# A column transform by one step of radix two, and the order of an opening: a float32 FFT and MoE kernel

## The chip, the cores and the metric

The kernel runs on one core of one Trainium2 chip. The metric is the device time in microseconds (us) of one execution; a kernel's time is the median of its runs. All arithmetic is in float32.

## The reference

```python
X = np.fft.fft(x, axis=1)          # x: (8, 3008, 256) float32
X = np.fft.fft(X, axis=2)
x = X.real.reshape(24064, 256)
h = x @ w_in                       # (256, 2048)
g = h * np.cos(h)
out = g @ w_out                    # (2048, 256)
```

A two-dimensional Fourier transform of each of 8 batches is taken, its real part goes through two matrix products with h cos(h) between them.

## The kernel before, in words

The transform along the 3008 rows is done in two halves with matrices of cosines and sines; the transform along the 256 columns is not applied to the data at all but to w_in, once, in the opening of the kernel. This folded w_in has two parts, WC (cosines, e = 0) and WS (sines, e = 1), 128 x 2048 each, and it takes the place of w_in for all 8 batches.

*The column transform.* w_in comes in four quarters n of 512 columns, each as two blocks of 128 rows side by side in a tile wr[n] (load_w, L241). For each quarter and each e, `weights` (L583) adds two matmuls into a PSUM tile pw: the upper 128 rows by one block of the constant matrix CS (256 x 256, load_cs, L235), the lower 128 rows by the other. `keep_weights` (L594) copies pw to WC or WS. Row 0 of WS is special: it belongs to column 128 of the transform. `send_wn` (L601) writes it to memory (tile wd) from ACT's queue and clears it with a memset on POOL (L602); `load_wn` (L605) reads it back as four columns of the tile wn, one value per partition.

*The first half* (first_half, L323 to L346) transforms rows of x into PSUM tiles pz with 64-column matmuls, one to partitions 0 to 63 and one to 64 to 127; ACT copies pz to zs (L346). store_z (L462) writes zs to memory (zd) and load_z (L493) reads it back in another layout (z2). For batches 1 to 7 the same is done by pair_half (L397, 64-column matmuls), keep_z (L408, ACT), fold_z (L415, POOL sums and differences of columns d and 256 - d) and store_pair, spread over the steps of the batch before.

*The second half* (second_half, L507) gives for a group of up to 256 frequencies the tile pb and, by ACT copies, pq, and its row nb.

*The main loop* has 384 steps (8 batches x 6 groups x 8 blocks fp of d_ff), each of two half-steps k. A half-step has on PE mm1 (L676, two matmuls with WC and WS into a PSUM tile H), on ACT seed (L657, writes H from nb and one column of wn before mm1 adds to it), act_e (L688), act_round (L704) and act_sin (L714), on DVE dve_h, dve_frac and dve_g. After both halves POOL makes sums (L734 to L741), and five half-steps later (LAG = 5) PE does mm2 (L767) of the step, seven matmuls with combinations of w_out (combine_w2, L642, on POOL in the opening). The seed of half-step k + 1 stands in half-step k. Half-steps 0 and 1 take their wn values through a matmul with wrow instead (seed_first, L663), so wn is first read by the seed of half-step 2 (columns 2 and 3 for half-steps 2 and 3); the second quarter's columns 4 to 7 are first read by the seed of half-step 4.

*Order.* The schedule is written out by hand: every engine does its instructions in the order of the program text, and a DMA is issued by the engine whose queue it is put on (SP, ACT or POOL), where a wait of the DMA also holds what is queued behind it. Only the waits between engines are put in by a framework. In the opening, all eight column transforms are placed by hand: three stand ahead of pb, one is split around the first mm1, and one stands in each of half-steps 1 to 4:

```python
if k in (1, 2, 3, 4):
    pw.append(weights(*((1, 2), (0, 2), (1, 3), (0, 3))[k - 1]))
```

keep_busy (L622) are matmuls without use at the very start.

Of the kernel before, what the change touches and what calls it, by code (L numbers as in the profile page):

```python
# [11 lines left out]
FP = mybir.dt.float32  # L12
# [21 lines left out]
def _consts():  # L34
# [53 lines left out]
                    if half == 0:  # L88
                        B[p, jj, 64 * e : 64 * e + 64] = blk[r, 0, 0]

    c = np.arange(ND)
    d = np.arange(128)
    ang = 2.0 * np.pi * np.outer(c, d) / ND
    CS = np.concatenate([np.cos(ang), -np.sin(ang)], axis=1) / TWO_PI
    CS[:, 128] = np.where(c % 2 == 0, 1.0, -1.0) / TWO_PI
# [34 lines left out]
def kernel(  # L130
# [86 lines left out]
                        in_=x_r[b, 15 * r : 15 * r + 32, 32 * q],  # L217
                    )

    CS = cpool.tile([128, 512], FP, tag="CS", name="CS")  # L220
    wr = {
        q: spool.tile([128, n], FP, tag=tag, bufs=m, name="wr")
        for q, tag, n, m in ((0, "r", 1024, 4), (1, "mr", 1792, 1), (2, "cb", 1792, 1), (3, "r", 1024, 4))
# [2 lines left out]
    def raw(q, i):  # L226
        return wr[q][:, 512 * i : 512 * i + 512]
# [4 lines left out]
    w2 = cpool.tile([128, 16 * ND], FP, tag="w2", name="w2")  # L232

    def load_cs(eng):
        eng.dma_start(  # L235
            out=CS.rearrange("p (i d) -> p i d", i=2),
            in_=CS_dr.ap().rearrange("(i p) d -> p i d", p=128),
        )

    def load_w(q, eng=nc.sync, i0=0, i1=2):  # L240
        eng.dma_start(  # L241
            out=wr[q][:, 512 * i0 : 512 * i1].rearrange("p (i f) -> p i f", f=512),
            in_=moe_w_in[128 * i0 : 128 * i1, 512 * q : 512 * q + 512].rearrange(
                "(i p) f -> p i f", p=128
            ),
        )

    def load_bj(c0, c1, eng=nc.sync):
        eng.dma_start(out=BJ[:, c0:c1], in_=B_dr.ap()[:, c0:c1])
# [13 lines left out]
    parts = (2, 3, 4, 5, 0, 1, 6, 7)  # L263
    for c in parts[:2]:
        load_x(c, 1, nc.scalar)
    WC = cpool.tile([128, NDFF], FP, tag="WC", name="WC")
    WS = cpool.tile([128, NDFF], FP, tag="WS", name="WS")
    wn = cpool.tile([128, 16], FP, tag="wn", name="wn")
# [42 lines left out]
    def first_half(c):  # L311

        fv = xfs.pop(c).rearrange("r (e c) -> r e c", e=2)[0:NX]
        LE, LO, LE0, LO0, LM = (L[0:NX, 64 * q : 64 * q + 64] for q in range(5))
        pz = psum("pz", "M")
        a = 128 if c == 0 else 0
        for e, (w, w0) in enumerate(((LE, LE0), (LO, LO0))):
            rows = slice(64 * e, 64 * e + 64)
            if a:
                nc.tensor.matmul(  # L320
                    pz[rows, 0:128], lhsT=w0, rhs=fv[:, e, 0:128], start=True, stop=True
                )
            nc.tensor.matmul(  # L323
                pz[rows, a:512],
                lhsT=w,
                rhs=fv[:, e, a:512],
                start=not a,
                stop=True,
                skip_group_check=True,
            )  # L330
        if a:
            nc.tensor.matmul(
                pz[64:128, 0:1], lhsT=LE0, rhs=fv[:, 1, 0:1], start=True, stop=True
            )
        nc.tensor.matmul(
            pz[64:128, a:512:128],
            lhsT=LM,
            rhs=fv[:, 1, a:512:128],
            start=True,
            stop=True,  # L340
        )
        p, q = divmod(c, 2)
        if q == 0:
            tag, n, m = ("xp", 4, XP * ND) if p in (0, 3) else ("zs", 2, 1024)
            zps[p] = spool.tile([128, m], FP, tag=tag, bufs=n, name="zs")
        nc.scalar.copy(out=zps[p][:, 512 * q : 512 * q + 512], in_=pz)  # L346

    zps = {}
    ws = {}
# [33 lines left out]
            )  # L383

    def fold_ends(e):
        lo, hi = xz[:, 1:128], xz[:, 255:128:-1]
        at = 129 if e else 1
        nc.gpsimd.tensor_tensor(
            out=xzf[:, at : at + 127], in0=lo, in1=hi, op=ALU.subtract if e else ALU.add
        )  # L390
        if e:
            small.append(dict(out=xzf[:, 0:129:128], in_=xz[:, 0:129:128]))

# [11 lines left out]
    def keep_z(b, p, q, pz):  # L405
        if q == 0:
            zrs[b, p] = spool.tile([128, XP * ND], FP, tag="xp", bufs=4, name="zr")
        nc.scalar.copy(out=zrs[b, p][:, 512 * q : 512 * q + 512], in_=pz)  # L408

    def fold_z(b, p, e):  # L410
        if e == 0:
            zfs[b, p] = spool.tile([128, 1024], FP, tag="zs", bufs=2, name="zs")
        zr = zrs[b, p][:, 0:1024].rearrange("y (i d) -> y i d", d=ND)
        zv = zfs[b, p].rearrange("y (e i d) -> y e i d", e=2, d=128)
        nc.gpsimd.tensor_tensor(  # L415
            out=zv[:, e, :, 1:128],
            in0=zr[:, :, 1:128],
            in1=zr[:, :, 255:128:-1],
            op=ALU.subtract if e else ALU.add,
        )  # L420

    def patch_z(b, p):
        zr = zrs[b, p][:, 0:1024].rearrange("y (i d) -> y i d", d=ND)
# [153 lines left out]
    def fold_weights(e, n, tag="M", copy=nc.scalar.copy):  # L577
        keep_weights(e, n, weights(e, n, tag), copy)

    def weights(e, n, tag="M", pw=None, both=(0, 1)):  # L580
        pw = pw or psum("pw", tag)
        for i in both:
            nc.tensor.matmul(  # L583
                pw,
                lhsT=CS[:, 256 * i + 128 * e : 256 * i + 128 * e + 128],
                rhs=raw(n, i),
                start=(i == 0),
                stop=(i == 1),
            )
        return pw  # L590

# [17 lines left out]
    class Step:  # L609
        pass  # L610

    VX = cpool.tile([128, 4 * 1024], FP, tag="VX", name="VX")
    ident = cpool.tile([128, 128], FP, tag="ident", name="ident")
    ones = cpool.tile([1, 128], FP, tag="ones", name="ones")
    nc.vector.memset(VX[:, 0:512], 1.0)
# [311 lines left out]
    load_cs(nc.sync)  # L927
    load_w(0)
    store_z(0, 0, 4)
    load_w(1, nc.gpsimd)  # L930
    store_z(3, 0, 4, (nc.sync, nc.scalar))
    load_bj(0, 512)
    for half in range(2):
        load_z(0, half, 0, 4, (nc.sync, nc.scalar))
    pw = [psum("pw", "H") for _ in range(2)]
    for e in (1, 0):
        weights(e, 0, pw=pw[e])
    keep_weights(1, 0, pw[1], copy_v)
    copy_v(out=wrow, in_=WS[0:1, 0:256])
    keep_weights(0, 0, pw[0], copy_v)  # L940
    send_wn(0)
    load_w2(0, 2, nc.gpsimd)
    load_w2(2, 4, nc.gpsimd)
    load_wn(0)
    load_w(2)
    fold_weights(1, 1, "M", copy_v)
    send_wn(1)
    for p in (1, 2):
        store_z(p, 4)
    load_wn(1)  # L950
    load_w(3)
    for p in (0, 3):
        store_z(p, 4)
    load_bj(512, 1024)
    for half in range(2):
# [2 lines left out]
    load_w2(6, 8)  # L958
    nc.sync.dma_start(out=L2, in_=L2_dr.ap())
    opening = {  # L960
        0: ((combine_w2, 0, 2), (combine_w2, 2, 4)),
        2: ((load_bj, 1024, NJ * 128),),
        3: ((combine_w2, 4, 6, 0, 2),),
        4: ((combine_w2, 4, 6, 2, 4),),
# [26 lines left out]
        h.H = psum("H", "H")  # L991
        nc.vector.memset(h.H[:, 0 : h.s.T], 0.25)
    second_half(0, 0)
    pw = [weights(0, 1, both=(0,))]
    steps[0].pq, steps[0].nb = ready[0, 0]
    for k in range(2 * n + LAG):
        t, u = divmod(k, 2)
# [4 lines left out]
        if cur:  # L1002
            if k % (2 * per) == 0:
                todo = transform(cur.s.b + 1) if cur.s.b + 1 < NB else {}
            if k >= AHEAD:
                mm1(cur, 0)
                act_e(cur)
            if k == 0:
                for h in (cur, nxt):
                    mm1(h, 0)  # L1010
                    seed_first(h)
                    act_e(h)
                    if h is cur:
                        weights(0, 1, pw=pw[0], both=(1,))
                spread_nb(0)
            if k < AHEAD - 1:
                mm1(cur, 1)
        pair = None if u else pairs.pop(t, None)
# [47 lines left out]
        if k in (1, 2, 3, 4, 5):  # L1066
            e, q = ((0, 1), (1, 2), (0, 2), (1, 3), (0, 3))[k - 1]
            keep_weights(e, q, pw[k - 1], copy_v)
        if k in (2, 5):
            send_wn(2 if k == 2 else 3)  # L1070
        elif k in (4, 7):
            load_wn(2 if k == 4 else 3, nc.scalar)
# [45 lines left out]
```

## Time and profile before

| | |
|---|---|
| median of 3 runs | 1926.72 us (1925.89 to 1927.38) |
| the profiled execution | 1926.21 us |
| its span, first to last instruction | 1924.4 us |
| mean granted clock of TensorE | 0.999 |
| busy: PE, DVE, ACT, POOL | 1914.2, 1465.8, 1493.0, 1427.7 us |
| first mm2 (L767) | 42.67 us |

Times are microseconds from the start of the span. PE is the matrix engine and PEld its weight loads, DVE the vector engine, ACT the scalar engine, POOL GpSimd, SP the engine that issues most DMAs; a name with a q (ACTq, SPq) is an engine's queue issuing a DMA or a wait. In rows, "x4" counts instruction records (a float32 matmul leaves two), "out<-in" gives the tiles by name, and an arrow with an engine names what an engine waited for.

### The profile page before, as it was taken

To read this page: it belongs to the slowest core of one execution; us is meant where nothing else is said; L and a number is where in the kernel's file an instruction comes from. 1 tells how busy PE (TensorE), PEld (TensorE's weight loads), DVE (VectorE), ACT (ScalarE), POOL (GpSimd) and SP (SyncE) were. 2 spreads that over 40 slices of the span, in tenths; PEclk is the share of its full clock that TensorE was granted. 3 is DMA by queue.
4 is the path that set the end of the run, shared out by engine and by line. 5 is a ranking of instruction groups with operands and counts; after the bars stand their busy time and mean duration, and the time that the engine had idled before them with its cause. 6 is when DMAs were issued, how large, how long until landed. Compare 5 with 4: busy or idle time off the path is not lost.

```text
span 1924.4 us, 29912 instructions
## 1 busy us (share of the span) xinstructions
PE 1914.2 (99%) x9240; PEld 1676.1 (87%) x9240; DVE 1465.8 (76%) x2538; ACT 1493.0 (78%) x3360; POOL 1427.7 (74%) x1705
## 2 busy tenths in 40 slices
PE   9999999999999999999999999999999999999998
PEld 5988899888988889888898888988889888898887
DVE  5777777777777777777777777777777777788787
ACT  3777778778777777778777887778777887778775
POOL 5878758887688776877668786788867788666775
PEclk9999999999999999999999999999999999999999
DMA  8612125011240113311142111511116111100001
GB/s 218 173 24 49 41 54 122 19 42 42 70 102 21 40 44 89 79 34 32 41 116 54 38 24 44 132 36 41 28 39 143 25 41 25 41 22 15 12 15 31
DMA packets 199251, 108.64 MB, mean 56 GB/s; under 512 B 113298, under 2 KB 182640, under 8 KB 198916
## 3 DMA queue, kind: packets, MB, share of 16 engines
q1 hardware_dynamic: 195092, 102.89, 22.7%
q0 software_dynamic: 864, 2.48, 0.4%
q10 hardware_dynamic: 3136, 1.36, 0.3%
q8 instruction: 75, 1.23, 0.3%
q14 instruction: 84, 0.69, 0.1%
HBM read 69.40 MB, written 48.40 MB: 61 GB/s over the span
## 4 chain that ended last, share of the span: by engine, by line
PE 87%; DMA 4%; SPq 4%; POOL 2%; DVE 1%; ACT 1%; issue 1%; DVEq 0%; POOLq 0%
PE M L767 52%; PE H L676 30%; PE pb L507 2%; DMA xp<-in_x_dram 2%; SPq L208 2%; PE pz L397 2%; SPq L905 1%; POOL xf L374 1%; PE pw L583 1%; DMA nb<-nd 1%; SPq L215 1%; DMA xp<-xr 0%; DMA nd<-pq 0%; POOL S L734 0%; PE pd L622 0%
## 5 line engine op out<-in xcount | busy, mean ns | idle before, releaser
L734 POOL TENSOR_TENSOR S<-r 128x512 f32<-128x512 f32 (+1 forms) x383 | 475.5, 1242 | 396.8 <-DVE r L718 344.1
L714 ACT ACTIVATE r<-r 128x512 f32<-128x512 f32 (+1 forms) x768 | 477.0, 621 | 254.8 <-DVE r L708 253.3
L708 DVE SCALAR_TENSOR_TENSOR r<-r,H 128x512 f32<-128x512 f32 (+1 forms) x768 | 519.0, 676 | 195.8 <-ACT r L704 169.0
L767 PE MATMUL M<-S,VX 128*128 128x256 f32 (+1 forms) x2304 | 619.8, 376 | 0.0
L718 DVE SCALAR_TENSOR_TENSOR r<-H,r 128x512 f32<-128x512 f32 (+1 forms) x768 | 519.1, 676 | 127.8 <-ACT r L714 86.7
L767 PEld LDWEIGHTS M<-S,VX 128*128 128x128 f32 x2304 | 435.4, 190 | 71.6 <-issue 22.7
L676 PE MATMUL H<-pq,WC 128*128 128x256 f32 (+1 forms) x1536 | 453.2, 377 | 0.1
L676 PE MATMUL H<-pq,WS 128*128 128x256 f32 (+1 forms) x1536 | 450.9, 375 | 0.0
L704 ACT ACTIVATE r<-H 128x512 f32<-128x512 f32 (+1 forms) x768 | 447.8, 583 | 0.2 <-DVE H L692 0.2
L692 DVE TENSOR_TENSOR H<-ew,H 128x256 f32<-128x256 f32 (+1 forms) x768 | 325.0, 423 | 113.6 <-PE H L676 52.9
L767 PE MATMUL M<-r,w 128*128 128x256 f32 (+1 forms) x1536 | 387.6, 375 | 0.0
L657 ACT ACTIVATE H<-nb,wn 128x256 f32<-128x256 f32 (+1 forms) x766 | 366.2, 478 | 1.8 <-DVE WS L594 0.6
L688 ACT ACTIVATE ew<-H 128x256 f32<-128x256 f32 (+1 forms) x768 | 288.0, 375 | 91.0 <-PE H L676 85.2
L767 PEld LDWEIGHTS M<-r,w 128*128 128x128 f32 x1536 | 300.3, 196 | 27.6 <-issue 0.5
L676 PEld LDWEIGHTS H<-pq,WS 128*128 128x128 f32 x1536 | 290.2, 190 | 34.6 <-issue 2.7
L676 PEld LDWEIGHTS H<-pq,WC 128*128 128x128 f32 x1536 | 279.7, 190 | 44.2 <-ACT H L657 7.7
L740 POOL TENSOR_TENSOR S<-S,r 128x256 f32<-128x256 f32 (+1 forms) x383 | 275.8, 720 | 30.0
L741 POOL TENSOR_TENSOR S<-r,S 128x256 f32<-128x256 f32 (+1 forms) x383 | 275.2, 719 | 30.0
L767 PE MATMUL M<-r,VX 128*128 128x256 f32 (+1 forms) x768 | 225.2, 375 | 0.0
L767 PE MATMUL M<-S,w 128*128 128x256 f32 (+1 forms) x768 | 225.2, 375 | 0.0
L767 PEld LDWEIGHTS M<-S,w 128*128 128x128 f32 x768 | 150.4, 196 | 14.6
L767 PEld LDWEIGHTS M<-r,VX 128*128 128x128 f32 x768 | 145.8, 190 | 14.6
(86 smaller groups left out, 913.5 us busy)
## 6 DMA issues: line engine op xcount, KB each, us to landing
out_dram<-ob SPq DMA_DIRECT2D x724, 32.0 KB
xp<-in_x_dram SPq DMA_DIRECT2D x119, 128.0 KB
xp<-xr SPq DMA_DIRECT2D x112, 128.0 KB
z<-zd SPq DMA_DIRECT2D x28, 384.0 KB
xr<-in_x_dram SPq DMA_DIRECT2D x14, 752.0 KB
zd<-zs SPq DMA_DIRECT2D x98, 96.0 KB
nb<-nd SPq DMA_DIRECT2D x39, 128.0 KB
wr<-in_moe_w_in_dram SPq DMA_DIRECT2D x3, 512.0 KB
```

The source lines that it names most:

```text
L657: nc.scalar.activation(out=h.H[:, 0:T], in_=s.nb[:, 0:T], func=AF.Copy, bias=0.25, scale=wn[:, f : f + 1])
L676: nc.tensor.matmul(h.H[:, 0:T], lhsT=W[:, 128 * f : 128 * f + 128], rhs=s.pq[:, e * T : e * T + T], start=False, stop=True, skip_group_che ...
L688: nc.scalar.mul(out=h.ew[:, 0:T], in_=h.H[:, 0:T], mul=2.0)
L692: nc.vector.tensor_tensor(out=h.H[:, T : 2 * T][:, ::-1], in0=h.ew[:, 0:T], in1=h.H[:, 0:T], op=ALU.subtract)
L704: nc.scalar.activation(out=r, in_=y, func=AF.Copy, bias=BIG, scale=1.0)
L708: nc.vector.scalar_tensor_tensor(out=r, in0=r, scalar=-BIG, in1=y, op0=ALU.add, op1=ALU.subtract)
L714: nc.scalar.activation(out=r, in_=r, func=AF.Sin, bias=0.0, scale=SIN_SCALE)
L718: nc.vector.scalar_tensor_tensor(out=r, in0=y, scalar=-0.25, in1=r, op0=ALU.add, op1=ALU.mult)
L734: tt(out=sv[:, 0:2], in0=qv[:, 1:2].to_broadcast([128, 2, T]), in1=qv[:, 0:4:3], op=ALU.subtract,)
L740: tt(out=sv[:, 2], in0=sv[:, 1], in1=gv[:, 0, 0], op=ALU.subtract)
L741: tt(out=sv[:, 3], in0=gv[:, 1, 0], in1=sv[:, 2], op=ALU.add)
L767: nc.tensor.matmul(acc[key][m // 2][:, 256 * (m % 2) : 256 * (m % 2) + T], lhsT=w, rhs=a, start=first, stop=s.fp == 7, skip_group_check=True,)
```

## The change

A transform of 256 points is done by one step of radix two. The two row blocks of each quarter of w_in are first added and subtracted (mix_weights: 8 sums or differences of 128 x 512, on DVE or POOL); even columns of the transform then need the sums alone, odd columns the differences alone. So each of the 16 matmuls of 128 x 512 with 128 columns of CS becomes one with 64 columns, the even to partitions 0 to 63 of pw and the odd to 64 to 127, and CS halves. The rows of WC and WS, and so the columns d of z, now stand with even d ahead of odd d: the copies of pz (zs and zr) read PSUM with a step of two, and fold_z and fold_ends are split by parity. The order of the opening changes as well: wr[1] is loaded by SP after the first BJ and ahead of the z loads, not by POOL; wr[2] and wr[3] are loaded one behind the other ahead of the remaining stores of z; both transforms of the second quarter (n = 1) stand behind pb, not ahead of it; its send_wn is issued by ACT in half-step 0 and its load_wn by ACT at the end of half-step 2, not by SP before the loop; two combine_w2 calls move from step 0 to step 1.

In the kernel after, the copy to zs is L344, second_half's pb L516, the matmuls of weights L607, send_wn L625, load_wn L629, seed L680, mm1 L699, the sums L757 and mm2 L790.

```diff
--- before.py
+++ after.py
@@ -88,8 +88,8 @@
                     if half == 0:
                         B[p, jj, 64 * e : 64 * e + 64] = blk[r, 0, 0]
 
-    c = np.arange(ND)
-    d = np.arange(128)
+    c = np.arange(128)
+    d = np.concatenate([np.arange(0, 128, 2), np.arange(1, 128, 2)])
     ang = 2.0 * np.pi * np.outer(c, d) / ND
     CS = np.concatenate([np.cos(ang), -np.sin(ang)], axis=1) / TWO_PI
     CS[:, 128] = np.where(c % 2 == 0, 1.0, -1.0) / TWO_PI
@@ -217,7 +217,7 @@
                         in_=x_r[b, 15 * r : 15 * r + 32, 32 * q],
                     )
 
-    CS = cpool.tile([128, 512], FP, tag="CS", name="CS")
+    CS = cpool.tile([128, 256], FP, tag="CS", name="CS")
     wr = {
         q: spool.tile([128, n], FP, tag=tag, bufs=m, name="wr")
         for q, tag, n, m in ((0, "r", 1024, 4), (1, "mr", 1792, 1), (2, "cb", 1792, 1), (3, "r", 1024, 4))
@@ -232,10 +232,7 @@
     w2 = cpool.tile([128, 16 * ND], FP, tag="w2", name="w2")
 
     def load_cs(eng):
-        eng.dma_start(
-            out=CS.rearrange("p (i d) -> p i d", i=2),
-            in_=CS_dr.ap().rearrange("(i p) d -> p i d", p=128),
-        )
+        eng.dma_start(out=CS, in_=CS_dr.ap())
 
     def load_w(q, eng=nc.sync, i0=0, i1=2):
         eng.dma_start(
@@ -263,6 +260,7 @@
     parts = (2, 3, 4, 5, 0, 1, 6, 7)
     for c in parts[:2]:
         load_x(c, 1, nc.scalar)
+    VX = cpool.tile([128, 4 * 1024], FP, tag="VX", name="VX")
     WC = cpool.tile([128, NDFF], FP, tag="WC", name="WC")
     WS = cpool.tile([128, NDFF], FP, tag="WS", name="WS")
     wn = cpool.tile([128, 16], FP, tag="wn", name="wn")
@@ -343,7 +341,10 @@
         if q == 0:
             tag, n, m = ("xp", 4, XP * ND) if p in (0, 3) else ("zs", 2, 1024)
             zps[p] = spool.tile([128, m], FP, tag=tag, bufs=n, name="zs")
-        nc.scalar.copy(out=zps[p][:, 512 * q : 512 * q + 512], in_=pz)
+        nc.scalar.copy(
+            out=zps[p][:, 512 * q : 512 * q + 512].rearrange("y (i o m) -> y i o m", o=2, m=64),
+            in_=pz.rearrange("y (i m o) -> y i o m", o=2, m=64),
+        )
 
     zps = {}
     ws = {}
@@ -383,11 +384,14 @@
             )
 
     def fold_ends(e):
-        lo, hi = xz[:, 1:128], xz[:, 255:128:-1]
-        at = 129 if e else 1
-        nc.gpsimd.tensor_tensor(
-            out=xzf[:, at : at + 127], in0=lo, in1=hi, op=ALU.subtract if e else ALU.add
-        )
+        at = 128 * e
+        for o, k in ((1, 64), (2, 1)):
+            nc.gpsimd.tensor_tensor(
+                out=xzf[:, at + k : at + (128 if o == 1 else 64)],
+                in0=xz[:, o:128:2],
+                in1=xz[:, 256 - o : 128 : -2],
+                op=ALU.subtract if e else ALU.add,
+            )
         if e:
             small.append(dict(out=xzf[:, 0:129:128], in_=xz[:, 0:129:128]))
 
@@ -405,19 +409,24 @@
     def keep_z(b, p, q, pz):
         if q == 0:
             zrs[b, p] = spool.tile([128, XP * ND], FP, tag="xp", bufs=4, name="zr")
-        nc.scalar.copy(out=zrs[b, p][:, 512 * q : 512 * q + 512], in_=pz)
+        nc.scalar.copy(
+            out=zrs[b, p][:, 512 * q : 512 * q + 512].rearrange("y (i o m) -> y i o m", o=2, m=128),
+            in_=pz.rearrange("y (i m o) -> y i o m", o=2, m=128),
+        )
 
     def fold_z(b, p, e):
         if e == 0:
             zfs[b, p] = spool.tile([128, 1024], FP, tag="zs", bufs=2, name="zs")
-        zr = zrs[b, p][:, 0:1024].rearrange("y (i d) -> y i d", d=ND)
-        zv = zfs[b, p].rearrange("y (e i d) -> y e i d", e=2, d=128)
-        nc.gpsimd.tensor_tensor(
-            out=zv[:, e, :, 1:128],
-            in0=zr[:, :, 1:128],
-            in1=zr[:, :, 255:128:-1],
-            op=ALU.subtract if e else ALU.add,
-        )
+        zr = zrs[b, p][:, 0:1024].rearrange("y (i o m) -> y i o m", o=2, m=128)
+        zv = zfs[b, p].rearrange("y (e i o m) -> y e i o m", e=2, o=2, m=64)
+        for o in range(2):
+            k = 1 - o
+            nc.gpsimd.tensor_tensor(
+                out=zv[:, e, :, o, k:64],
+                in0=zr[:, :, o, k:64],
+                in1=zr[:, :, o, 127 : 64 - o : -1],
+                op=ALU.subtract if e else ALU.add,
+            )
 
     def patch_z(b, p):
         zr = zrs[b, p][:, 0:1024].rearrange("y (i d) -> y i d", d=ND)
@@ -577,15 +586,30 @@
     def fold_weights(e, n, tag="M", copy=nc.scalar.copy):
         keep_weights(e, n, weights(e, n, tag), copy)
 
-    def weights(e, n, tag="M", pw=None, both=(0, 1)):
+    def mixed(n, o):
+        if n in (1, 2):
+            at = 0 if o else 1024
+            return wr[n][:, at : at + 512]
+        at = 512 if n == 0 else 768
+        return VX.rearrange("p (v c) -> p v c", v=4)[:, 2 * o : 2 * o + 2, at : at + 256]
+
+    def mix_weights(n, o, eng):
+        to = mixed(n, o)
+        a, b = raw(n, 0), raw(n, 1)
+        if n not in (1, 2):
+            a, b = (t.rearrange("p (v c) -> p v c", v=2) for t in (a, b))
+        eng.tensor_tensor(out=to, in0=a, in1=b, op=ALU.subtract if o else ALU.add)
+
+    def weights(e, n, tag="M", pw=None):
         pw = pw or psum("pw", tag)
-        for i in both:
+        for o in range(2):
+            at = 128 * e + 64 * o
             nc.tensor.matmul(
-                pw,
-                lhsT=CS[:, 256 * i + 128 * e : 256 * i + 128 * e + 128],
-                rhs=raw(n, i),
-                start=(i == 0),
-                stop=(i == 1),
+                pw[64 * o : 64 * o + 64],
+                lhsT=CS[:, at : at + 64],
+                rhs=mixed(n, o),
+                start=True,
+                stop=True,
             )
         return pw
 
@@ -609,7 +633,6 @@
     class Step:
         pass
 
-    VX = cpool.tile([128, 4 * 1024], FP, tag="VX", name="VX")
     ident = cpool.tile([128, 128], FP, tag="ident", name="ident")
     ones = cpool.tile([1, 128], FP, tag="ones", name="ones")
     nc.vector.memset(VX[:, 0:512], 1.0)
@@ -927,29 +950,25 @@
     load_cs(nc.sync)
     load_w(0)
     store_z(0, 0, 4)
-    load_w(1, nc.gpsimd)
+    mix_weights(0, 0, nc.vector)
+    mix_weights(0, 1, nc.gpsimd)
     store_z(3, 0, 4, (nc.sync, nc.scalar))
     load_bj(0, 512)
+    load_w(1)
     for half in range(2):
         load_z(0, half, 0, 4, (nc.sync, nc.scalar))
-    pw = [psum("pw", "H") for _ in range(2)]
-    for e in (1, 0):
-        weights(e, 0, pw=pw[e])
-    keep_weights(1, 0, pw[1], copy_v)
+    fold_weights(1, 0, "H", copy_v)
     copy_v(out=wrow, in_=WS[0:1, 0:256])
-    keep_weights(0, 0, pw[0], copy_v)
     send_wn(0)
+    fold_weights(0, 0, "H", copy_v)
     load_w2(0, 2, nc.gpsimd)
     load_w2(2, 4, nc.gpsimd)
     load_wn(0)
     load_w(2)
-    fold_weights(1, 1, "M", copy_v)
-    send_wn(1)
-    for p in (1, 2):
-        store_z(p, 4)
-    load_wn(1)
     load_w(3)
-    for p in (0, 3):
+    for o in range(2):
+        mix_weights(2, o, nc.gpsimd)
+    for p in (1, 2, 0, 3):
         store_z(p, 4)
     load_bj(512, 1024)
     for half in range(2):
@@ -958,7 +977,8 @@
     load_w2(6, 8)
     nc.sync.dma_start(out=L2, in_=L2_dr.ap())
     opening = {
-        0: ((combine_w2, 0, 2), (combine_w2, 2, 4)),
+        0: ((combine_w2, 0, 2),),
+        1: ((combine_w2, 2, 4),),
         2: ((load_bj, 1024, NJ * 128),),
         3: ((combine_w2, 4, 6, 0, 2),),
         4: ((combine_w2, 4, 6, 2, 4),),
@@ -991,7 +1011,10 @@
         h.H = psum("H", "H")
         nc.vector.memset(h.H[:, 0 : h.s.T], 0.25)
     second_half(0, 0)
-    pw = [weights(0, 1, both=(0,))]
+    for o in range(2):
+        mix_weights(1, o, nc.vector)
+    fold_weights(1, 1, "M", copy_v)
+    pw = []
     steps[0].pq, steps[0].nb = ready[0, 0]
     for k in range(2 * n + LAG):
         t, u = divmod(k, 2)
@@ -1011,8 +1034,11 @@
                     seed_first(h)
                     act_e(h)
                     if h is cur:
-                        weights(0, 1, pw=pw[0], both=(1,))
+                        pw.append(weights(0, 1))
                 spread_nb(0)
+                send_wn(1)
+                for o in range(2):
+                    mix_weights(3, o, nc.gpsimd)
             if k < AHEAD - 1:
                 mm1(cur, 1)
         pair = None if u else pairs.pop(t, None)
@@ -1066,6 +1092,8 @@
         if k in (1, 2, 3, 4, 5):
             e, q = ((0, 1), (1, 2), (0, 2), (1, 3), (0, 3))[k - 1]
             keep_weights(e, q, pw[k - 1], copy_v)
+        if k == 2:
+            load_wn(1, nc.scalar)
         if k in (2, 5):
             send_wn(2 if k == 2 else 3)
         elif k in (4, 7):
```

## The prediction

> **What bounds the kernel now.** I read the page first, then the stretches of time, then the chain that ended last in its opening 48 us, then ACT's and SP's timelines there.
>
> ```profile
> PE 1914.2 (99%) x9240; PEld 1676.1 (87%) x9240; DVE 1465.8 (76%) x2538; ACT 1493.0 (78%) x3360; POOL 1427.7 (74%) x1705
> ...
> core 0: us, PE busy (x) PEld busy (x) DVE busy (x) ACT busy (x) POOL busy (x), PEclk, DMA share, GB/s
> 0.00:20.00 20.00, 17.47 (x66) 8.03 (x66) 10.55 (x18) 5.88 (x10) 11.11 (x25) 1.00 0.76 213
> 20.00:40.00 20.00, 18.78 (x60) 10.23 (x61) 8.92 (x19) 7.95 (x20) 8.19 (x12) 1.00 0.74 222
> 40.00:60.00 20.00, 20.00 (x104) 18.49 (x102) 15.03 (x28) 14.25 (x35) 16.04 (x22) 1.00 0.97 237
> 200.00:1900.00 1700.00, 1699.64 (x8245) 1503.04 (x8245) 1312.81 (x2270) 1345.07 (x3032) 1270.83 (x1501) 1.00 0.22 50
> ```
>
> From about 40 us to the end PE has no gap: 1699.64 of 1700 us. So the change can move the end only by moving the moment from which PE is never late again, or by putting new stalls into the steady part. I take the first mm2 (L767) at 42.67 us as that moment; later than that is later at the end, one for one. The chain ahead of it:
>
> ```profile
> 16.45 4.57 DMA wr<-in_moe_w_in_dram
> 21.02 0.14 issue
> 21.15 5.40 PE pw L583 x12
> 26.55 0.02 issue
> ...
> 33.53 1.72 PE pw L583 x4
> 35.25 0.76 PE H L676 x4
> 36.01 1.72 PE pw L583 x4
> 37.73 0.91 PE H L676 x4
> 38.64 1.72 PE pw L583 x4
> 40.36 0.76 PE H L676 x4
> 41.12 1.72 PE pw L583 x4
> 42.83 1.14 PE M L767 x6
> ```
>
> A float32 matmul is two records here, so "x4, 1.72" is one column transform of a quarter for one parity: two matmuls of 0.86 us. Four of these lie between mm1s (L676), and PE does not wait. The same stretch on ACT and SP:
>
> ```profile
> 36.32 0.58 ACT L714 ACTIVATE r<-r 128x450 f32<-128x450 f32 x1
> 37.22 0.22 ACTq L601 DMA_DIRECT2D wd<-WS  x1
> 37.49 0.45 ACT L657 ACTIVATE H<-nb,wn 128x225 f32<-128x225 f32 x1 [0.59 <-DVE WS L594]
> ...
> 41.23 0.43 ACTq L605 DMA_DIRECT2D wn<-wd  x1
> ...
> 32.40 0.38 SPq L605 DMA_DIRECT2D wn<-wd  x1
> ```
>
> The seed at 37.49 is that of half-step 4, the first that reads columns 4 to 7 of wn. Its load was issued by SP at 32.40; the trace has its last packet at 36.97, so the seed was not held by it.
>
> **The change part by part.**
>
> *Shorter pw.* A pair of 64-column matmuls of 512 columns on the two halves of the partitions runs side by side: in L323 (8.77 to 9.69 us) two take 0.92 us from start to end. With about 0.1 us to go into and out of that shape on each side, I estimate 1.19 us per quarter and parity instead of 1.72, a saving of 0.53. Before, three of the eight transforms (the 5.40 us) stood ahead of pb (L507) and five behind it, 5 x 1.72 = 8.6 us. Now two (n=0) stand ahead and six behind, since n=1 is moved back: 6 x 1.19 = 7.1 us. What lies ahead of pb saves nothing by itself, since pb needs z: the four z loads landed at 24.43, 25.45, 25.63 and 26.08 us, and pb began at 26.38. So at most 8.6 - 7.1 = 1.5 us of the saving is on the path.
>
> *Mixes.* Eight 128x512 sums and differences. n=0: 0.69 us on DVE (as L734's last on DVE) beside 1.25 on POOL (383 of L734 take a mean of 1242 ns), between wr0's landing and the first pw. wr0 lands some 1 us earlier without wr1's transfer on POOL's queue beside it (18.00 to 23.06) and with half of CS. Then pw is done at about 22.8, well ahead of z: free. n=1 on DVE while PE does pb: 2 x 0.69, hidden if wr1 is there. n=2 on POOL: wr2 landed at 31.81, so 2 x 1.25 behind gives 34.3, and the pair for it ends at about 35.3; before, that pw ended at 35.09. So up to the third half-step nothing is gained. n=3 stands on POOL behind the memset of row n=1 and has until about 38.
>
> *wr1 on SP, ahead of the z loads.* Its issue costs about 0.5 us of SP, which then waits for zd anyway. But 512 KB now cross in the very time in which z is stored and read back. Bounds: 0 (the same bytes by about 26 us, at the 222 GB/s of that stretch) and 1.3 us (half of 512 KB at 200 GB/s ahead of z). I take 0.4.
>
> *Strided reads.* The copies L344 read PSUM in steps of two. No row shows this. Bounds: 0, as POOL's L642 takes 728 ns with a step of two and 731 without, and 0.43 us, which doubling the cost per element would add (128x512 586 ns, 128x225 348 ns: 0.83 ns each). One such copy is on the path to z. I take the lower end, as the POOL row is near. [...] The copies in the steady part (56 at L408) have ACT's 22% idle time for cover; 56 x 0.43 = 24 us are 1.2% of the span.
>
> *fold_z in twice as many pieces.* 112 of about 0.73 us (128x256 on POOL) for 56 of 1.27: 0.2 us more each pair of pieces. POOL waits 344 us in total for DVE ahead of L734 and the sums are ready 2.3 us or more ahead of their mm2, so nothing; if uncovered, 56 x 0.2 = 11 us.
>
> *One PE instruction stream otherwise unchanged, ACT +1 issue.* send_wn(1) is now issued by ACT ahead of the seed of half-step 2: 0.25 us, in front of mm1 there. The pair of n=1 ahead of half-step 0 costs 0.2 us more than the 0.86 us that stood there.
>
> *The load of wn's second quarter.* This is the large term. send_wn(1) was issued at 27.30 and landed at 32.39. It now comes at about 32.4, behind the copy of nb. Its load is no longer on SP at once, but on ACT at the end of half-step 2. ACT reaches that place where the sin at 36.32 ends, 36.9, plus the front's delays: 0.4 + 0.25 + 0.2 = 0.85, about 37.75. wd1 must have landed: by the four times seen (1.4, 5.1, 3.1 and 5.4 us) at 33.8 to 37.8, so hardly later. The load takes 2.11 us on light queues (25.86 to 27.97), and 4.57, 5.39 and 4.29 under load (32.40, 41.23 and 48.66). The DMA share from 40 us is 0.97, and stores and w2 are issued no later than before: I take 4.7 and keep 2.1 to 5.4. So wn is there at 42.45. The seed of half-step 4 waits for that on ACT; queued behind it are the round of half-step 3, then e, sin and the next seed; mm1 of half-step 4 waits for the seed, and all of PE behind mm1.
>
> From seed to first mm2 it was 42.67 - 37.49 = 5.18 us. Two pw lie in between, 2 x 0.53 shorter: 4.1. First mm2 at 42.45 + 4.1 = 46.55, that is 3.9 us later. wn's third and fourth quarters follow the same order with the same distances, so no second stall.
>
> **The sum.** The profiled execution took 1926.21 us (span 1924.4), 0.5 under the median of 1926.72. 1926.21 + 3.9 = 1930.1; on the median 1930.6. With the small uncovered pieces (boundaries of pairs, POOL closer to its limits) I put 0.2 on top: 1930.8. With the load at 2.1 us it would be 1928.2, with 5.4 it is 1931.5.
>
> **The rivals.**
>
> *wn comes in time, or nearly* (not slower). If the load takes 2.1 us and z is not delayed, the seed is at about 39.4 and the first mm2 at 43.5: 1927.5 to 1928.2. For: 2 KB took 2.11 us at 25.86. Against: every other load of wn took over 4.2 us, and this one goes out when w2, BJ and z are in flight. It decides below a load of about 4.4 us.
>
> *The clock falls* (slower still). PE is idle from the last pair of n=0, about 22.8, to pb at 26.4 to 26.8, some 3.6 to 4 us, where before it had pw. The longest idle time before this was 1.57 us (19.6 to 21.15), with the granted clock at 1.00 after it; at the start it took to 7.3 us, 5.8 us of work, until records went from 0.85 to 0.43 us. If the clock halved, the first 2 to 3 us of work after pb would take as much longer: 2.5 us later at half-step 2 and at the wn load: 1930.8 + 2.5 = 1933.3. For: the gap is new and over twice the longest seen. Against: no row shows the clock falling. [...]
>
> *The saving comes through* (faster). z is there 1.7 us earlier because wr1 no longer runs beside the stores (store at 20.44 landed at 23.49, 3.05 us; at the 2 us of the z loads it would be a us sooner), wn comes in time, and 1.5 us of shorter pw count: 1926.7 - 3.2 = 1923.5, and with 0.7 more from the pairs' overlap 1922.8. Against: needs all three, and wr2 at 31.81 caps it.
>
> *Pairs do not run side by side.* Each pw then takes 1.72 as before plus the mixes, seed to mm2 stays 5.18: 1931.9. L323's and L397's rows speak against.
>
> **Chances.** 0.2% of the time, 3.85 us, is about what a measurement can tell from no change: faster is below 1922.9, slower above 1930.6. Late wn: 0.50, of which 0.31 above the bound and 0.19 below; wn in time: 0.17, same; clock: 0.22, slower; saving comes through: 0.09, of which 0.07 beyond the bound; pairs one after the other: 0.02, slower. Together faster 0.07, same 0.38, slower 0.55. The range runs from wn in time, 1927.0, to the clock's fall with a load of 5.4 us, 1933.3 + 0.7 and its spread, 1934.8.
>
> **What would show it.** In the trace after: an idle time of ACT ahead of the seed of half-step 4 of some 4 us put down to wn's DMA, and PE idle behind it; the first mm2 near 46.6; pw groups of near 1.2 us; PE idle from about 22.8 to 26.5, with the records after it at 0.43 us per 512 columns (clock kept) or 0.85 (fallen); PE without gaps from 47 us on. A first mm2 before 43, or gaps of PE at the fold_z steps after 85 us, would prove me wrong.

## The result, and the profile after

| | before | after |
|---|---|---|
| median | 1926.55 us (1925.89 to 1927.98, 8 runs) | 1932.13 us (1931.01 to 1936.48, 8 runs) |
| ratio | | 1.0031, 95% interval 1.0020 to 1.0042 |
| the profiled execution | 1926.21 us | 1936.48 us |
| its first mm2 | 42.67 us | 52.62 us |
| its time less its first mm2 | 1883.5 us | 1883.9 us |

The change made the kernel 5.6 us slower; 1930.8 was forecast, in a range of 1927.0 to 1934.8. The profiled execution of the kernel after is the slowest of its eight, 10.3 us above that of before, so a second trace was taken (again, below: 1934.31 us, first mm2 at 50.41). The last row of the table says where the loss lies: all ahead of the first mm2. The stretches of the kernel after:

```profile
20.00:40.00 20.00, 16.26 (x43) 7.02 (x44) 6.52 (x13) 4.08 (x11) 7.04 (x8) 0.70 0.72 216
40.00:60.00 20.00, 16.36 (x67) 10.61 (x64) 12.74 (x24) 10.53 (x26) 15.29 (x21) 0.88 0.74 170
...
200.00:1900.00 1700.00, 1698.62 (x8246) 1500.99 (x8245) 1310.14 (x2269) 1344.13 (x3032) 1278.39 (x1563) 1.00 0.22 50
```

Two things differ from before. PE is busy for 16.3 and 16.4 us in the two stretches instead of 18.8 and 20.0, and the granted clock (third column from the right) is 0.70 and 0.88 where it was 1.00. Behind 200 us PE is as full as before to 1 us (1698.62 of 1700 us, before 1699.64). PE in time, kernel after:

```profile
21.10 3.05 PE L607 MATMUL pw<-VX,CS 128*64 128x512 f32 x8 [1.21 <-DVE VX L601]
26.74 1.13 PE L516 MATMUL pb<-BJ,z 128*128 128x128 f32 x8 [2.59 <-DMA z<-zd]
27.80 1.98 PE L607 MATMUL pw<-wr,CS 128*64 128x512 f32 x4
...
42.17 1.08 PE L607 MATMUL pw<-wr,CS 128*64 128x512 f32 x4
43.18 0.65 PE L699 MATMUL H<-pq,WS 128*128 128x225 f32 x2
47.47 0.65 PE L699 MATMUL H<-pq,WC 128*128 128x225 f32 x2 [3.65 <-ACT H L680]
48.05 1.78 PE L607 MATMUL pw<-VX,CS 128*64 128x512 f32 x4
...
52.62 1.03 PE L790 MATMUL M<-r,w 128*128 128x225 f32 x4
```

A pair of transforms' halves takes 1.08 us at full clock (42.17) and 1.98 at half clock (27.80). The trace's clock records give 0.50 from 27.81 to 41.47 and again from 48.29 to 51.71. The 3.65 us ahead of 47.47 are the wait that the prediction held likeliest. ACT shows its end:

```profile
42.34 0.41 ACTq L629 DMA_DIRECT2D wn<-wd  x1
...
46.97 0.45 ACT L680 ACTIVATE H<-nb,wn 128x225 f32<-128x225 f32 x1 [3.87 <-DMA wn<-wd]
```

So the seed of half-step 4 did wait for wn's second quarter, and the clock did fall as well: the likeliest case and the rival of a falling clock came together.

### The profile page after: what moved, and what is told of

Same layout as the page of the kernel before. It is cut to its first block, busy times and chain, and to the rows that moved or that the text cites. A ratio compares the mean times of both kernels' runs of the same rounds, so it can differ in the third digit from the quotient of the medians.

```text
span 1934.7 us, 29997 instructions
## 1 busy us (share of the span) xinstructions
PE 1917.8 (99%) x9240; PEld 1674.2 (87%) x9240; DVE 1466.6 (76%) x2541; ACT 1491.9 (77%) x3360; POOL 1442.3 (75%) x1779
## 4 chain that ended last, share of the span: by engine, by line
PE 86%; DMA 5%; SPq 4%; POOL 2%; DVE 1%; ACT 1%; issue 1%; ACTq 0%; POOLq 0%; DVEq 0%
PE M L790 51%; PE H L699 30%; DMA xp<-in_x_dram 3%; PE pb L516 2%; PE pz L401 2%; SPq L208 2%; SPq L928 1%; DMA nb<-nd 1%; POOL xf L375 1%; SPq L215 1%; DMA xp<-xr 0%; DMA nd<-pq 0%; POOL S L757 0%; PE pz L321 0%; DVE r L731 0%
## 5 line engine op out<-in xcount | busy, mean ns | idle before, releaser
L757 POOL TENSOR_TENSOR S<-r 128x512 f32<-128x512 f32 (+1 forms) x383 | 475.0, 1240 | 391.7 <-DVE r L741 342.2
L790 PE MATMUL M<-S,VX 128*128 128x256 f32 (+1 forms) x2304 | 619.8, 376 | 0.0
L790 PEld LDWEIGHTS M<-S,VX 128*128 128x128 f32 x2304 | 435.4, 190 | 71.6 <-issue 22.7
L699 PE MATMUL H<-pq,WC 128*128 128x256 f32 (+1 forms) x1536 | 455.1, 378 | 3.6 <-ACT H L680 3.6
L699 PE MATMUL H<-pq,WS 128*128 128x256 f32 (+1 forms) x1536 | 452.7, 377 | 0.0
L790 PE MATMUL M<-r,w 128*128 128x256 f32 (+1 forms) x1536 | 387.7, 375 | 0.0
L680 ACT ACTIVATE H<-nb,wn 128x256 f32<-128x256 f32 (+1 forms) x766 | 366.4, 478 | 5.1 <-DMA wn<-wd 3.9
L790 PEld LDWEIGHTS M<-r,w 128*128 128x128 f32 x1536 | 300.2, 196 | 27.9 <-issue 0.8
L699 PEld LDWEIGHTS H<-pq,WC 128*128 128x128 f32 x1536 | 280.5, 190 | 50.0 <-ACT H L680 12.0
L699 PEld LDWEIGHTS H<-pq,WS 128*128 128x128 f32 x1536 | 290.9, 190 | 37.4 <-issue 1.7
L790 PE MATMUL M<-r,VX 128*128 128x256 f32 (+1 forms) x768 | 225.2, 375 | 0.0
L790 PE MATMUL M<-S,w 128*128 128x256 f32 (+1 forms) x768 | 225.2, 375 | 0.0
L790 PEld LDWEIGHTS M<-S,w 128*128 128x128 f32 x768 | 150.4, 196 | 14.6
L790 PEld LDWEIGHTS M<-r,VX 128*128 128x128 f32 x768 | 145.8, 190 | 14.6
```

The source lines that it names most:

```text
L680: nc.scalar.activation(out=h.H[:, 0:T], in_=s.nb[:, 0:T], func=AF.Copy, bias=0.25, scale=wn[:, f : f + 1])
L699: nc.tensor.matmul(h.H[:, 0:T], lhsT=W[:, 128 * f : 128 * f + 128], rhs=s.pq[:, e * T : e * T + T], start=False, stop=True, skip_group_che ...
L757: tt(out=sv[:, 0:2], in0=qv[:, 1:2].to_broadcast([128, 2, T]), in1=qv[:, 0:4:3], op=ALU.subtract,)
L790: nc.tensor.matmul(acc[key][m // 2][:, 256 * (m % 2) : 256 * (m % 2) + T], lhsT=w, rhs=a, start=first, stop=s.fp == 7, skip_group_check=True,)
```

## The experiments

All times are medians, with those of the kernel before, taken on the same chip, behind them; a ratio is formed from all runs of both, not from the two medians, and stands with its 95% interval. "First mm2" is that of the profiled execution.

**again: the kernel after once more.** No edit.

> The kernel after, unchanged, for a second trace: how long the clock stays down and how long half-step 4 waits. Both theories: 1931.0 to 1932.5 us. Theory clock (PE idle ahead of pb lets the clock fall): granted 0.50 again from about 1 us after pb's start, for 3 to 14 us. Theory late wn alone: ACT idle ahead of the seed of half-step 4 by 3.5 to 4.5 us whatever the clock does.

Measured: 1932.26 us (before 1926.80), ratio 1.0029 (1.0020 to 1.0038). Its profiled execution has half clock from 28.38 to 42.03, again 13.65 us, and none behind the wait:

```profile
46.75 0.65 PE L699 MATMUL H<-pq,WC 128*128 128x225 f32 x2 [2.83 <-ACT H L680]
47.32 1.08 PE L607 MATMUL pw<-VX,CS 128*64 128x512 f32 x4
```

From the seed of half-step 4 (46.24) to the first mm2 (50.41) it is 4.17 us at full clock, where before it was 5.18.

**late: one move alone in the kernel before.**

```diff
-    load_wn(1)
     load_w(3)
 ...
+        if k == 2:
+            load_wn(1, nc.scalar)
         if k in (2, 5):
             send_wn(2 if k == 2 else 3)
```

> The kernel before with one move alone: load_wn(1) from SP (issued at 32.40) to ACT at the end of half-step 2. The term of 3.9 us in the prediction, priced by itself. If it is right: the load issued near 37, wn there 3.5 to 5 us later, first mm2 at 45.5 to 47, 1929.5 to 1931 us, 2 to 3 us more where the wait lets the clock fall. If a load there is hidden: 1926 to 1927.5 us.

Measured: 1931.66 us (before 1926.91), ratio 1.0023 (1.0012 to 1.0033). First mm2 at 48.41. ACT of this kernel:

```profile
36.45 0.41 ACTq L605 DMA_DIRECT2D wn<-wd  x1
...
41.53 0.45 ACT L657 ACTIVATE H<-nb,wn 128x225 f32<-128x225 f32 x1 [4.57 <-DMA wn<-wd]
```

and its PE:

```profile
42.04 0.76 PE L676 MATMUL H<-pq,WC 128*128 128x225 f32 x2 [3.88 <-ACT H L657]
```

The seed comes at 41.53 instead of 37.49, 4.04 us later. PE then stands still for 3.88 us, and the clock is at half from 42.45 to 45.86, which takes another 1.70 us (5.74 in all at the first mm2, 5.70 in the time of the profiled execution). One 2 KB load in another place costs 4.8 us by the medians, where the whole change costs 5.6.

**fill: PE kept busy ahead of pb.**

```diff
+    pd = psum("pd", "M")
+    for _ in range(3):
+        keep_busy(pd, 512, True)
     second_half(0, 0)
```

> The kernel after with three idle-time matmuls (keep_busy, 512 columns, no result used) between the last pair of n=0 and pb, 2.6 us of PE work in the 2.6 us gap. If the gap lets the clock fall: granted 1.00 from 20 to 43 us, half-step 2 some 5 us earlier than at half clock, first mm2 near 46.5, 1929.5 to 1930.5 us; the later wait at half-step 4 may still let it fall once. If the gap is not the cause: clock still 0.50 after pb, 1932 us.

Measured: 1932.41 us (before 1926.80), ratio 1.0027 (1.0016 to 1.0039). First mm2 at 48.53. PE:

```profile
24.03 2.84 PE L645 MATMUL pd<-VX 128*128 128x512 f32 x6
27.81 1.13 PE L516 MATMUL pb<-BJ,z 128*128 128x128 f32 x8 [0.93 <-DMA z<-zd]
...
42.11 1.12 PE L699 MATMUL H<-pq,WC 128*128 128x225 f32 x2 [2.98 <-ACT H L680]
43.16 1.98 PE L607 MATMUL pw<-VX,CS 128*64 128x512 f32 x4
```

The fall behind pb is gone (the clock is 1.00 to 41.41), so the gap there was its cause. Half-step 4 starts 5.4 us sooner than in the kernel after. But it still waits for wn, and that wait now brings the fall: half clock from 41.41 to 48.23. The time is no better. Either wait can bring a fall: that ahead of pb in after and again, that at half-step 4 in fill and late.

**early: the second quarter's wn sent and loaded early.**

```diff
     fold_weights(1, 1, "M", copy_v)
+    send_wn(1)
+    for p in (1, 2):
+        store_z(p, 4)
+    load_wn(1)
+    for p in (0, 3):
+        store_z(p, 4)
 ...
-                send_wn(1)
 ...
-        if k == 2:
-            load_wn(1, nc.scalar)
```

> The kernel after with only the order of the second quarter's wn changed: send_wn(1) right behind its transform (ahead of half-step 0), load_wn(1) on SP between the second and the third store as before the change. If the late wn costs by itself: no wait at the seed of half-step 4, 3 to 4.5 us less, 1927.7 to 1929 us, with the clock still falling after pb. If the wait is only the place where the delay of the slow clock shows: 1931 to 1932.5 us.

Measured: 1929.45 us (before 1926.80), ratio 1.0020 (1.0011 to 1.0029). No wait at the seed of half-step 4; 2.8 us of the 5.5 are back. In the profiled execution (1936.03, one of two of eleven near 1936) the clock fell in the gap ahead of pb, at 26.46, and stayed at half for 17.07 us.

**both: fill and early together.**

> Both edits: idle-time matmuls ahead of pb and the second quarter's wn sent and loaded early. If the two causes are all: first mm2 at 41.5 to 42.7, 1925.5 to 1927.0 us, equal to the kernel before within 0.05% or slightly faster (the shorter pairs bring at most 1.5 us). If the pairs, the mixes on POOL or the split folds cost something of their own: above 1928 us.

Measured: 1929.33 us (before 1926.80), ratio 1.0011 (1.0003 to 1.0020). First mm2 at 44.12, still 1.5 us late, and from there on 1.7 us more than before. So the two causes are not all. In this trace PE waited 1.84 us for wr0 and its mix (19.61 to 21.45), and the clock was at half from 22.34 to 25.75; and the next quarter's wn was late in turn:

```profile
ACT H L680 <- DMA wn<-wd: 1.2, 1, 1.2
```

This is the seed of half-step 8: the load of the third quarter was issued at 43.69 and landed at 50.62.

**order: the change's order without its arithmetic.** The kernel before with the second quarter behind pb, the loads, send_wn(1), load_wn(1) and combine_w2 placed as after; transforms with 128 columns as before.

> The kernel before with only the order of the change: both transforms of the second quarter behind pb, wr1 on SP ahead of the z loads, wr2 and wr3 back to back, send_wn(1) in half-step 0, load_wn(1) on ACT at the end of half-step 2, combine_w2 moved. The column transforms stay as they were (128 columns, two row blocks). If the order makes the loss: a wait of 3 to 4 us ahead of the seed of half-step 4, first mm2 at 47 to 49, 1931.5 to 1934 us, no less than the kernel after. If the radix step itself (mixes, pairs, strided copies, split folds) makes it: 1926 to 1928 us.

Measured: 1934.70 us (5 runs; before 1926.87), ratio 1.0040 (1.0027 to 1.0053). PE:

```profile
27.04 1.99 PE L507 MATMUL pb<-BJ,z 128*128 128x128 f32 x8 [3.05 <-DMA z<-zd]
...
43.75 0.65 PE L676 MATMUL H<-pq,WC 128*128 128x225 f32 x2 [1.85 <-ACT H L657]
```

Both waits are there without any sum or difference, so the order alone makes a loss no smaller than that of the whole change. Its median is 2.6 us above that of after, but the two intervals overlap and its five runs spread from 1932.10 to 1937.90 us: that the radix step made the loss smaller is not shown.

**layout: even columns ahead of odd, and nothing else.** CS in that order, the copies L344 and those of keep_z with a step of two, fold_z and fold_ends in pieces.

> The kernel before with even columns of z and of the folded weights ahead of odd, and nothing else: columns of CS in that order, copies that read PSUM with a step of two, fold_z and fold_ends in twice as many pieces. As predicted (nothing uncovered): within 0.5 us of the kernel before, from first mm2 to the end as long as before to 0.5 us. If strided reads or the pieces cost: 1928 us or more, with a gap on PE in each batch.

Measured: 1926.73 us (before 1926.91), ratio 0.9999 (0.9990 to 1.0008). Its groups, and two of the kernel before:

```profile
L415 POOL TENSOR_TENSOR zs<-zr 128x508 f32<-128x508 f32 x56 | 71.0, 1268 | 0.0
L408 ACT COPY zr<-pz 128x512 f32<-128x512 f32 x56 | 32.2, 576 | 16.8 <-PE pz L397 12.6 <-issue 3.5 <-POOL xm L367 0.7
...
L426 POOL TENSOR_TENSOR zs<-zr 128x252 f32<-128x252 f32 x112 | 78.9, 726 | 0.0
L414 ACT COPY zr<-pz 128x512 f32<-128x512 f32 x56 | 32.2, 575 | 17.8 <-PE pz L403 12.6 <-POOL xm L370 5.2
L346 ACT COPY zs<-pz 128x512 f32<-128x512 f32 x8 | 4.7, 585 | 10.6 <-PE pz L335 9.0 <-DMA zd<-zs 0.9 <-DVE xf L299 0.7
```

The copies with a step of two take 575 and 585 ns, where they took 576 and 586. The pieces take 726 ns each, 79 us of POOL in place of 71. PE gets one gap of 0.23 us in each of six batches, 1.4 us in all where it had 0.4; from the first mm2 to the end it is 1884.0 us, 0.5 more than before, which the medians do not show.

**pairs: the radix step in the order of before.** wr1 on POOL, one transform of the second quarter ahead of pb, wn and wr3 as before, mixes but one on DVE.

> The radix step alone in the order of the kernel before (wr1 on POOL, one transform of the second quarter ahead of pb, its wn sent and loaded as before, wr3 behind it); all mixes but one of the first quarter on DVE. If the order made the loss: no wait ahead of the seed of half-step 4, clock kept, 1925.5 to 1927.5 us; the gain is held to under 1 us because wr3 lands at about 38. If the radix step costs: 1928 us or more.

Measured: 1932.32 us (before 1926.87), ratio 1.0029 (1.0018 to 1.0040). The radix step in this order loses as much as the change. That does not settle what the arithmetic costs by itself, because the placement of its mixes brought a wait of its own. DVE:

```profile
39.93 2.26 DVE L601 TENSOR_TENSOR VX<-wr 128x512 f32<-128x512 f32 x2 [1.07 <-DMA wr<-in_moe_w_in_dram]
```

The mixes of the last quarter stand on DVE ahead of the copy of the third quarter's WS and wait for wr3, which landed at 39.90; ACT's send_wn(2) waits for that copy, the seed of half-step 4 stands behind it (43.38, 3.91 us of ACT idle put down to the copy), and PE idles 3.86 us. The clock fell there (43.01) and once before, ahead of the first pairs (22.53).

**best: the radix step with wr3 and load_wn(1) sooner.** As pairs, but wr3 behind wr2, load_wn(1) ahead of the stores, one mix of the last quarter on POOL.

> The radix step with an order meant to use it: as the last, but wr3 loaded right behind wr2 and load_wn(1) on SP ahead of all four remaining stores, one mix of the last quarter on POOL. If shorter pairs can reach the end once wr3 and wn are in time: first mm2 at 41 to 42, 1925 to 1926.5 us. If the queues of the opening only pass the delay on: a wait of 1 us or more ahead of the seed of half-step 4 or 8, 1926.5 to 1929 us.

Measured: 1929.96 us (before 1926.87), ratio 1.0016 (1.0007 to 1.0025). No fall of the clock in its trace, and yet the first mm2 is at 44.05: PE waits 1.29 us for the first mix, 0.93 for that of n=1, 0.82 ahead of the first mm1 (nothing lies between pb and it any more) and 1.39 at half-step 4.

**tall and tall2: one-row matmuls made 128 rows high.** wrow and ones as tiles of 128 rows with zeros below the first, in the kernel after; run twice.

> The kernel after with its one-row matmuls (wrow in seed_first, ones in spread_nb: six records each way in the first two half-steps) made 128 rows high with zeros below the first row: the same time at full clock, the same result. In every trace so far a stretch at half clock ended only behind a 3.41 us window that held no one-row matmul and little idle time. If those matmuls keep the clock down: the half-clock stretch behind pb lasts 3.4 or 6.8 us, not 13.7, half-step 2 ends 3 to 5 us sooner, 1929.5 to 1931.5 us. If not: 13.7 us again and 1932 us.

> The kernel with 128-row matmuls in place of one-row ones once more, for a second trace: in the first the clock fell at 22 us, ahead of them. If one-row matmuls keep the clock down and it falls behind pb this time: half clock for 3.4 or 6.8 us; if not: 13.7 us.

Measured: tall 1932.65 us (before 1927.02), ratio 1.0030 (1.0020 to 1.0040); tall2 one run, 1931.72. In neither trace did the clock fall behind pb: in tall it fell at 21.99 and at 42.47, in tall2 at 42.26, each time for 3.41 us. So the question that they were made for stays open. What they show is below, at the windows.

**hybrid: the first two quarters as before, the last two by sums and differences.** CS whole; the second load of w_out behind the memset of n=1 on POOL (it still went at 28.33), row 0 of the third quarter cleared behind the first sums, load_wn(1) on SP ahead of the stores.

> The first two quarters transformed as before the change (two 128-column matmuls, no mix, one ahead of pb and one split around the first mm1, CS whole), the last two by sums and differences: mixes of the third on DVE, of the fourth on DVE and POOL; wr3 right behind wr2, the second load of w_out (two blocks fp) held back on POOL, load_wn(1) on SP ahead of the stores, the clearing of row 0 of the third quarter behind the first sums. If the shorter pairs reach the end where PE is the bound and no mix, wn or idle time stands ahead: four transforms at 1.01 instead of 1.72 us, first mm2 at 40 to 41.5, 1924.5 to 1926.5 us. If wn's round trips set the pace again: waits ahead of the seeds of half-steps 4 and 8, 1927 to 1929 us.

Measured: 1926.97 us (before 1927.02), ratio 1.0000 (0.9991 to 1.0009). PE:

```profile
34.02 1.08 PE L620 MATMUL pw<-wr,CS 128*64 128x512 f32 x4
...
36.18 0.65 PE L716 MATMUL H<-pq,WC 128*128 128x225 f32 x2 [0.51 <-ACT H L697]
36.76 1.08 PE L620 MATMUL pw<-wr,CS 128*64 128x512 f32 x4
...
38.95 0.65 PE L716 MATMUL H<-pq,WC 128*128 128x225 f32 x2 [0.54 <-ACT H L697]
```

The clock is kept and no seed waits for wn, but the first mm2 is at 42.90, no sooner than before. A pair saves 0.71 us itself, about 0.5 with the mm1s around it (below), so some 2 us for four. z landed at 26.77 instead of 26.07, and PE now waits for the seeds of half-steps 3 and 4, 1.05 us in all: in a stretch in which PE was the bound, it now waits for ACT. No kernel here beats the kernel before.

## Why the prediction held, and where it did not

*What sets the end.* The first mm2, one for one: right for the kernel after. In the traces of after, again, fill, late and order the time less the first mm2 is 1883.5 to 1883.9 us, as before. It is no rule for the others. In both, best, tall and tall2 it is 1.7 to 2.6 us more: the load of the third quarter took 6.9 to 8.0 us there, and the seed of half-step 8 waited 1.2 to 2.2 us for it. In early it is 3.3 us more: POOL stood still for 8.0 us until that quarter's row was stored, and the sums and mm2 stood behind it. In hybrid it is 1.6 more without such a wait. "No second stall" thus held in the two traces of the kernel after, but tall and tall2 have the same order and had one.

*The late wn.* The step was right and well sized. The 3.9 us of the forecast are not to be set beside the 4.04 of late, though: 3.9 is what was left of a seed 4.96 us later (42.45 instead of 37.49) behind the shorter pairs, and late has neither these nor the 0.85 us by which the load was to be issued later. For late the prediction's own terms give 36.9 + 4.7 - 37.49 = 4.1, and 4.04 came. The load took 5.1 us there and 4.6 and 3.8 in the two traces of after, 3.5 in fill (4.7 taken). From the seed to the first mm2 4.1 was forecast and 4.17 measured.

*The clock.* This is the step that failed, in two ways. It was given 0.22 and one place, the gap ahead of pb; in the trace of before the granted clock stays at 1.00 from 7.31 us to behind the last matmul, so the chance and the length of a fall were the author's estimate. The other place was not seen: the forecast wait for wn is itself an idle time of PE of 3 to 4 us, so the term of 3.9 us brought its own fall, 1.70 us in late and, as 6.93 us from seed to first mm2 instead of 4.17 show, 2.8 in fill. A fall at the one place or the other (or both) is in both traces of the kernel after and in late, fill, order, tall and tall2. And a fall behind pb was priced at 2.5 us, for 2 to 3 us of half clock, a length that no run shows: the shortest stretch in any trace is 3.41 us, and 13.65 us were at half clock in both traces of after: the load at the end of half-step 2 was issued at 42.34 and 42.43, against 38.05 in fill, where pb came a us later. But both traces are of long executions. Of nineteen executions of the kernel after (eight and the eleven of again), the four with a mean granted clock of 0.995 or 0.996 took 1934.31 to 1936.48 us, the two traced ones among them; the other fifteen, at 0.997 or 0.998, took 1930.54 to 1933.47. The other variants' traces at 0.997 and 0.998 have 3.41 to 10.24 us at half clock ahead of the last matmuls. So the median of 1932.13, 1.3 us above the forecast, probably holds a shorter fall, as tall2 does; no execution of the kernel after near its median was traced. The likeliest case was right in kind. That the number came so near is in part luck, since it left out a fall that every trace with the wait shows except again and order; the range held because it reached to this rival.

The prediction read the longest idle time of PE before as 1.57 us (19.6 to 21.15); the row at 21.15 in the kernel before has 1.37. The argument holds with either number.

*Shorter pw.* 1.19 us estimated with the change of shape (0.92 and 0.1 on each side would be 1.12; no run shows the 0.1 by itself). From a pair to the next matmul 1.01 was measured (in fill 35.15 to 36.16), 0.71 less than before. But the mm1s around the pairs take longer, the two ahead of the last pair 1.07 us in again (48.33 to 49.40), 0.76 before (40.19 to 40.95): from the seed of half-step 4 to the first mm2 two pairs saved 5.18 - 4.17 = 1.01 us. That is 0.5 each, as forecast.

*Mixes.* The one of the first quarter on POOL was put at 1.25 us and took 1.76:

```profile
20.40 1.76 POOL L601 TENSOR_TENSOR VX<-wr 128x512 f32<-128x512 f32 x1 [2.24 <-DMA wr<-in_moe_w_in_dram]
```

The four later ones on POOL took 2.60 and 2.48 us for two each (fill), about what was put. It was not the first one alone: in every trace a mix on POOL that began just behind one on DVE took 1.76 or 1.77 us, the later one at 38.05 in best too, and every other 1.25 to 1.27. The two mixes of the first quarter were priced as if they ran side by side. wr0 landed at 20.33, 0.69 sooner than before and not 1 us. So the pairs of n=0 ended at 24.15, not 22.8, and the gap ahead of pb was 2.59 us, not 3.6 to 4. It was enough for the clock all the same.

*z.* 0.4 us later was taken, 0.6 measured (26.65 against 26.07).

*Strided reads and pieces.* Nothing in the medians, as said (layout). Yet the pieces are not quite free: fold_ends takes 0.66 us on POOL in two pieces (302.03 in layout) where one took 0.46 (301.71 before), and ahead of pz PE waits 0.23 us for POOL in each of six batches. ACT's copies from PSUM with a step of two took 575 and 585 ns, against 576 and 586 without: of the two bounds it was the lower one, 0.

*The rivals.* "The saving comes through" and "pairs do not run side by side" both fell: the pairs run side by side (1.01 us from a pair to the next matmul, 1.72 before), and not one variant turned them into time. "wn in time" did not happen; made to happen in early it gave 1929.45, 1.3 us above the upper end worked out for it. In the trace of early the clock still fell and the next quarter was late; but the fall of 17.07 us goes with the two executions near 1936, and the other nine took 1928.62 to 1930.85.

## What to carry to other kernels

Where PE's end is set by the moment from which it never waits, a small load that is moved can cost more than all the arithmetic that is saved (in late 4.8 us for one of 2 KB, where two shorter pairs saved 1.01): price each load by the longest time seen under load (5.4 us before, and up to 8.0 in tall), and look for what is queued behind its reader. Count an idle time of PE twice, for itself and for the clock behind it (3.88 and 1.70 us in late), also where the forecast itself adds the wait. And look at which engine waits next once the bound one is faster: in hybrid the time saved on PE came back as waits for ACT (1.05 us) and for z (landed 0.70 us later).

## What the hardware showed

In these traces the granted clock changes in steps of one length. All stretches at half clock between the first change and the last matmuls of these fourteen traces are 3.41, 6.83, 13.65 or 17.07 us, that is 1, 2, 4 or 5 windows of 3.41 us, and windows counted on from a kernel's first change fit all later ones: in after 27.81, 41.47, 48.29 and 51.71 us are 6, 10, 12 and 13 windows behind 7.33. With PE's idle time in each window (records of the traces):

```
window with the fall behind it   idle in it, us
after 24.4, 44.9                 2.34, 2.59
again 25.0                       1.85
fill 38.0                        2.28
early 23.0                       2.27
both 18.9                        1.84
order 23.7                       3.05
pairs 19.1, 39.6                 2.16, 2.99
tall 18.6, 39.1                  1.82, 2.73
late 39.0                        3.01
tall2 38.8                       2.43
window without a fall, most idle
tall2 21.8, 25.2                 1.79, 1.77
tall 52.7                        1.68
order 40.7                       1.85
```

Some 1.8 us without matmuls in one window, about half of it, stood ahead of every fall (1.82 in tall the least), and the length of a gap alone did not decide: 3.56 us without work ahead of pb in tall2 lay across two windows, 1.79 and 1.77, and the clock held, while 1.84 us in one window brought it down in both. The border is not sharp: one window with 1.85 us (order, 40.7) held. So the place of a gap in the grid goes into what it costs. It differs from run to run (the first change is at 7.33 us in after and at 4.49 in again), and may well be a part of the spread of the kernel after.

How long the clock stays down is not settled. Nine windows at half clock without any idle time ended without the clock's return (three each in after, again and early), and all nine held one-row matmuls (wrow, ones); every window without idle time and without them ended with its return. That is a correlation; the runs made to test it did not fall there.
